# Thresholded attention into a tanh-shrink MLP on one core: rows 4p+c per partition, dense blocks by batch, output transposes later, weight casts behind their loads, threshold shift on VectorE

## The chip, the cores and the metric

One NeuronCore of a Trainium2 chip runs the whole program; the other cores are idle. The metric is the device time of one execution in microseconds (us), as the median of several runs. The engines are named as the profile names them: PE is the matrix engine (TensorE; PEld are its weight loads), DVE is VectorE, ACT is ScalarE, POOL is GpSimd, SP is the engine that issues most of the DMA transfers. Each engine works through its own queue in order, and semaphores tie the queues together.

## The reference, cut to what matters

```python
# q, k, v: 8 batches x 8 heads x 576 x 64, f32; tau = 0.02
scores = q @ k^T / 8                                # 576 x 576 for each head
thresh = max(scores, axis=-1) - tau
scores = where(scores >= thresh, scores, -1e9)
attn   = exp(scores - max(scores)); attn /= sum(attn) + 1e-9
x      = (attn @ v), heads side by side             # 4608 tokens x 512
h      = x @ w_in                                   # 512 -> 2048
out    = (h - tanh(h)) @ w_out                      # 2048 -> 512, f32
```

## The kernel before, in words

**Attention.** Two heads of a batch form a *pair*; there are 32 pairs, four to a batch. A pair has nine *tiles* of 128 query rows: four of the first head, a shared one with the last 64 rows of both heads (j = 4, kind "M"), four of the second. `load` brings q, k and v of a pair in f32; `split` turns q and k into a high and a low fp16 part (on POOL, for the first pair on ACT and DVE); `turn` transposes them on PE and copies the result from PSUM on DVE. For k a second matrix kS with the high and low halves swapped is made from kT by two DMAs.

For each tile: `scores` runs two groups of matmuls (with kT and kS) into one of two PSUM buffers, DVE scales the result into `sc` and takes the row maximum `mx`, POOL makes the shift `nb = tau - mx` (L226); `kink` on ACT (L240) applies a Prelu with a steep slope, which sends all below the threshold far down; `weights` transposes the result z on PE into the single PSUM buffer psZ (L256), and ACT takes the exponential into pT (L266); `attend` multiplies pT with v, on every second tile for two tiles at once, with a column of ones beside v that gives the row sums. `norm` (DVE, L314 and L315) divides, for the first head after tile 4 and for the second after tile 8, into `osb`. `emit_x` (L320) transposes `osb` on PE (psX, L324 and L331), in the same PSUM buffer as psZ, and DVE copies it into xT (L336).

**Dense layers.** Tokens are worked in nine blocks of 512. `hidden` computes 128 of the 2048 hidden columns for a block (four matmuls, tanh on ACT, the difference g on DVE); `project` adds a quarter of an output tile (four matmuls). `layers(m)` lists the 16 hidden steps of block m and the 16 projecting steps of block m-1.

**What sets the order.** There is no scheduler: the loop from L430 writes every engine's queue by hand. Step s does, in this order, the scores of tile s+3, the kink of s+1, the weights of s, then the dense steps that are due, `attend` of s-1, `norm`, `emit_x`, then loads, splits and turns of the next pair, and (in the first batch) a piece of the weights. At the first tile of the second and of each later batch a list of dense steps is taken up (16 in the first such batch, 32 in the later ones) and spread over the 36 tiles of the batch. In the first batch there are none. The last blocks run after the loop, without attention beside them: the tail.

The weights, 16 pieces of 128 x 1024 f32, go through two buffers: `w_load` issues the DMA and at once writes the cast to bf16 into POOL's queue (L417), one piece at each of the tiles 3 to 8 of a pair until all are there.

Of the kernel before, what the change touches and what calls it, by code (L numbers as in the profile page):

```python
# [10 lines left out]
BF16 = mybir.dt.bfloat16  # L11
# [7 lines left out]
def kernel(  # L19
# [32 lines left out]
    W = 2 * S  # L52
    AHEAD = 3

    MB = 512
    NMB = NT // MB
    MS = MB // P

    const = ctx.enter_context(tc.tile_pool(name="const", bufs=1))
    ident_f16 = const.tile([P, P], FP16, name="ident_f16")  # L60
# [1 line left out]
    ident_bf = const.tile([P, P], BF16, name="ident_bf")  # L62
    make_identity(nc, ident_bf)

    xT = const.tile([P, DM_C, NT], BF16, name="xT")
    w_in_sb = const.tile([P, DM_C, d_ff], BF16, name="w_in_sb")
    w_out_sb = const.tile([P, DF_C, d_model], BF16, name="w_out_sb")

# [36 lines left out]

    raws = {}

    def load(p):
        b, h0 = p // HPAIR, 2 * (p % HPAIR)
        for t, src in (("k", k), ("q", q)):  # L110
            r = raw_pool.tile([P, 10, D], F32, name=f"{t}raw", tag=t)
            for hh in range(2):
                nc.sync.dma_start(
                    out=r[:, 5 * hh : 5 * hh + 4, :],
                    in_=src[b, h0 + hh, 0:512, :].rearrange("(c p) d -> p c d", p=P),
                )
                nc.sync.dma_start(
                    out=r[64 * hh : 64 * hh + 64, 4, :], in_=src[b, h0 + hh, 512:S, :]
                )
            raws[p, t] = r  # L120
        r = raw_pool.tile([P, 10, D], F32, name="vraw", tag="v")
        for hh in range(2):
            nc.sync.dma_start(
                out=r[:, 4 * hh : 4 * hh + 4, :],
                in_=v[b, h0 + hh, 0:512, :].rearrange("(c p) d -> p c d", p=P),
            )
        rem = v[b, h0 : h0 + 2, 512:S, :].rearrange("h s d -> s h d")
        nc.sync.dma_start(out=r[0:64, 8:10, :], in_=rem)
        nc.sync.dma_start(out=r[64:P, 8:10, :], in_=rem)
        raws[p, "v"] = r  # L130
# [36 lines left out]
    def turn(p, t):  # L167
        hl = hls.pop((p, t))
        ps = ps_big.tile([P, W], FP16, name=f"ps_{t}", tag="big")
        for c in range(TPP):  # L170
            nc.tensor.matmul(  # L171
                out=ps[:, c * P : (c + 1) * P],
                lhsT=hl[:, c, :, :].rearrange("p a d -> p (a d)"),
                rhs=ident_f16, is_transpose=True, start=True, stop=True,
            )
        m = qk_pool.tile([P, W], FP16, name=f"{t}T", tag=t)
        nc.vector.tensor_copy(out=m, in_=ps)  # L177
        mats[p, t] = m
        if t == "k":
            sw = qk_pool.tile([P, W], FP16, name="kS", tag="ks")  # L180
            nc.sync.dma_start(out=sw[0:D, :], in_=m[D:P, :])
            nc.sync.dma_start(out=sw[D:P, :], in_=m[0:D, :])
            mats[p, "ks"] = sw
# [10 lines left out]
    def scores(i):  # L194
        p, j = divmod(i, TPP)
        qT, kT, kS = mats[p, "q"], mats[p, "k"], mats[p, "ks"]
        ps = ps_big.tile([P, 1024], F32, name="psS", tag="big")
        main, rem, lo = slice(0, 512), slice(512, 576), 0
        if kind(j) == "B":
            main, rem, lo = slice(512, 1024), slice(448, 512), 448  # L200
        if j == 4:
            for n, kk in enumerate((kT, kS)):
                for dst, srcs in ((main, MAIN), (rem, REM)):
                    for hh in range(2):
                        nc.tensor.matmul(  # L205
                            out=ps[64 * hh : 64 * hh + 64, dst],
                            lhsT=qT[:, REM[hh]], rhs=kk[:, srcs[hh]],
                            start=(n == 0), stop=(n == 1),
                        )
        else:  # L210
            hh = int(j > 4)
            lhs = qT[:, j * P : (j + 1) * P]
            for n, kk in enumerate((kT, kS)):
                for dst, src in ((main, MAIN[hh]), (rem, REM[hh])):
                    nc.tensor.matmul(  # L215
                        out=ps[:, dst], lhsT=lhs, rhs=kk[:, src],
                        start=(n == 0), stop=(n == 1),
                    )
        sc = sc_pool.tile([P, S], F32, name="sc")
        mx = st_pool.tile([P, 1], F32, name="mx", tag="mx")  # L220
        nc.vector.tensor_scalar(  # L221
            out=sc, in0=ps[:, lo : lo + S], scalar1=SC, scalar2=None,
            op0=ALU.mult, op1=ALU.max, accum_out=mx,
        )
        nb = st_pool.tile([P, 1], F32, name="nb", tag="nb")
        nc.gpsimd.tensor_scalar(  # L226
            out=nb, in0=mx, scalar1=-1.0, scalar2=tau, op0=ALU.mult, op1=ALU.add
        )
        scs[i] = sc, nb
# [90 lines left out]
    def emit_x(p):  # L320
# [12 lines left out]
                is_transpose=True, start=True, stop=True,  # L333
            )
        b = p // HPAIR
        nc.vector.tensor_copy(out=xT[:, p % HPAIR, b * S : (b + 1) * S], in_=ps)  # L336


    gs = {}
# [1 line left out]
    def hidden(m, n, ps):  # L341
        if n == 0:
            gs[m] = g_pool.tile([P, DF_C, MB], BF16, name="g")
        for c in range(DM_C):
            nc.tensor.matmul(  # L345
                out=ps, lhsT=w_in_sb[:, c, n * P : (n + 1) * P],
                rhs=xT[:, c, m * MB : (m + 1) * MB],
                start=(c == 0), stop=(c == DM_C - 1),
            )
        th = t_pool.tile([P, MB], F32, name="th")  # L350
        nc.scalar.activation(out=th, in_=ps, func=ACT.Tanh)  # L351
        nc.vector.scalar_tensor_tensor(  # L352
            out=gs[m][:, n, :], in0=th, scalar=-1.0, in1=ps,
            op0=ALU.mult, op1=ALU.add,
        )

    def project(m, ms, part, ps, last):
# [5 lines left out]
        if part == 3:  # L363
# [2 lines left out]
                nc.scalar.copy(out=yo, in_=ps)  # L366
            else:
                nc.vector.tensor_copy(out=yo, in_=ps)  # L368
            t0 = m * MB + ms * P
            nc.sync.dma_start(out=out[t0 : t0 + P, :], in_=yo)  # L370

    def layers(m, tail):

# [24 lines left out]
    def w_pieces():  # L398
        for w, sb, n in ((moe_w_in, w_in_sb, DM_C), (moe_w_out, w_out_sb, DF_C)):
# [3 lines left out]
            for i in range(8):  # L403
                yield flat, src, i, cols, w.shape[1]

    def w_load(piece):
        flat, src, i, cols, width = piece
        wt = wt_pool.tile([P, cols], F32, name="wt", tag="wt")
# [4 lines left out]
        else:  # L413
            r = width // cols
            s = src[:, i // r, (i % r) * cols : (i % r + 1) * cols]
            nc.sync.dma_start(out=wt, in_=s)
        nc.gpsimd.tensor_copy(out=flat[:, i * cols : (i + 1) * cols], in_=wt)  # L417


    load(0)  # L420
# [3 lines left out]
        turn(0, t)  # L424
    split_v(0)
    pieces = w_pieces()

    todo, stage = [], 0

    for s in range(-AHEAD, NTILE + 2):  # L430
        p, j = divmod(max(s, 0), TPP)
        if 0 <= s < NTILE and j == 0 and p % HPAIR == 0 and p >= HPAIR:
            assert not todo
            todo = layers(stage, False)
            share = len(todo) / (HPAIR * TPP)
            done, stage = 0.0, stage + 1
        if s + AHEAD < NTILE:
            scores(s + AHEAD)
# [2 lines left out]
        if 0 <= s < NTILE:  # L441
            weights(s)
            if todo:
# [3 lines left out]
                while todo and done >= 1:  # L447
                    todo.pop(0)()
                    done -= 1
        if 0 <= s - 1 < NTILE:  # L450
            attend(s - 1)
            pp, jj = divmod(s - 1, TPP)
# [1 line left out]
                norm(pp, 0)  # L454
            if jj == 8:
                norm(pp, 1)
                emit_x(pp)
        if 0 <= s < NTILE:
            if j == 0 and p + 2 < NPAIR:
                load(p + 2)  # L460
            if p + 1 < NPAIR:
# [6 lines left out]
                    turn(p + 1, "k")  # L468
                if j == 4:
                    turn(p + 1, "q")  # L470
            if p < HPAIR and j >= 3:
                piece = next(pieces, None)
                if piece:
                    w_load(piece)
# [42 lines left out]
```

## Time and profile before

| | |
|---|---|
| median of 3 runs | 702.17 us (701.99 to 703.81) |
| the profiled execution | 701.69 us, its span 699.9 us |
| PE busy | 609.4 us, 87% |
| ACT busy | 462.1 us, 66% |
| DVE busy | 422.5 us, 60% |
| POOL busy | 272.0 us, 39% |
| mean granted PE clock | 0.975 of full |

The span runs from the first to the last instruction. A busy time is the time in which an engine executed at least one instruction, over the whole span, so over stages with quite different limits; matmuls are pipelined and their ends are modelled, so that an engine with a busy share near 100% need not be at its peak. In a row of the order of time, what stands in brackets at the end is how long that engine had stood idle and what released it. In the rows of waits, the engine on the left stood still until the instruction on the right had ended; where an engine has nothing to do anyway, such a wait costs nothing.

### The profile page before, as it was taken

What the parts mean: (1) busy time and instruction counts of PE and PEld (TensorE: products, weight loads), DVE (VectorE), ACT (ScalarE), POOL (GpSimd) and SP (SyncE); (2) the same over time, 40 slices, a digit from 0 to 9 for tenths busy, and PEclk for the clock granted to TensorE, in tenths of its full rate; (3) what the DMA queues carried; (4) which work ended last, traced back from release to release, by engine and by line L of the source; (5) the groups of instructions that cost most, each with busy time, mean ns of one, the idle gap of its engine ahead of it and who ended that gap; (6) DMA issues with size and microseconds to landing.
All of it is one profiled execution on the core that took longest, in us unless ns stands there. A gap on an engine that the chain in (4) does not pass through costs nothing.

```text
span 699.9 us, 16371 instructions
## 1 busy us (share of the span) xinstructions
PE 609.4 (87%) x6112; PEld 366.5 (52%) x6112; DVE 422.5 (60%) x985; ACT 462.1 (66%) x761; POOL 272.0 (39%) x597
## 2 busy tenths in 40 slices
PE   1765688888999999999999999999999999999997
PEld 1443455555555555555555555555555555554443
DVE  1534456666666666666676766666666666654440
ACT  1555578777777777777777777777777777763330
POOL 2564655444444444433434344444444443200000
PEclk9978789999999999999999999999999999999999
DMA  5567643332133332323232333333332332100102
GB/s 118 134 182 215 180 95 85 72 70 63 27 86 85 87 85 72 78 72 86 69 78 68 83 84 87 85 85 88 85 81 67 83 77 54 33 16 31 46 30 76
DMA packets 134543, 57.70 MB, mean 82 GB/s; under 512 B 122688, under 2 KB 122688, under 8 KB 134464
## 3 DMA queue, kind: packets, MB, share of 16 engines
q1 hardware_dynamic: 134464, 56.66, 32.4%
q8 instruction: 48, 0.79, 0.5%
q14 instruction: 31, 0.25, 0.1%
HBM read 37.75 MB, written 9.44 MB: 67 GB/s over the span
## 4 chain that ended last, share of the span: by engine, by line
PE 69%; ACT 9%; DVE 8%; DMA 4%; issue 3%; POOL 3%; SPq 2%; POOLq 0%; DVEq 0%; ACTq 0%
PE psY L359 17%; PE psH L345 15%; PE psS L215 12%; PE psZ L256 9%; ACT th L351 3%; ACT pT L266 3%; PE psS L205 3%; ACT z L240 3%; PE psHt L345 2%; PE psO L300 2%; DVE yo L368 2%; DMA wt<-in_moe_w_in_dram 2%; PE ps_k L171 2%; PE psX L324 2%; DVE osb L315 2%
## 5 line engine op out<-in xcount | busy, mean ns | idle before, releaser
L266 ACT ACTIVATE pT<-psZ 128x512 f16<-128x512 bf16 (+1 forms) x288 | 184.2, 640 | 120.2 <-PE psZ L256 118.8
L240 ACT ACTIVATE z<-sc,nb 128x576 bf16<-128x576 f32 x288 | 221.5, 769 | 38.2 <-POOL nb L226 37.9
L221 DVE TENSOR_SCALAR_CACHE_REDUCE sc<-psS 128x576 f32<-128x576 f32 x288 | 214.9, 752 | 38.6 <-PE psS L215 15.6
L226 POOL TENSOR_SCALAR nb<-mx 128x1 f32<-128x1 f32 x288 | 54.8, 190 | 301.0 <-DVE sc L221 198.5
L352 DVE SCALAR_TENSOR_TENSOR g<-th,psH 128x512 bf16<-128x512 f32 x124 | 85.3, 688 | 114.5 <-ACT th L351 114.5
L359 PE MATMUL psY<-w_out_sb,g 128*128 128x512 bf16 x576 | 145.5, 379 | 0.0
L256 PE MATMUL psZ<-ident_bf,z 128*128 128x128 bf16 x1280 | 121.6, 223 | 27.0 <-ACT pT L266 25.5
L345 PE MATMUL psH<-xT,w_in_sb 128*128 128x512 bf16 x496 | 128.2, 381 | 0.5 <-DVE g L352 0.5
L256 PEld LDWEIGHTS <-z 128*128 128x128 bf16 x1280 | 80.8, 99 | 71.4 <-issue 28.7
L215 PE MATMUL psS<-kS,qT 128*128 128x512 f16 (+1 forms) x512 | 107.6, 293 | 5.3 <-DMA kS<-kT 5.2
L215 PE MATMUL psS<-kT,qT 128*128 128x512 f16 (+1 forms) x512 | 107.8, 293 | 3.6 <-DVE kT L177 1.9
L215 PEld LDWEIGHTS <-qT 128*128 128x128 f16 x1024 | 74.9, 99 | 63.9 <-issue 6.5
L351 ACT ACTIVATE th<-psH 128x512 f32<-128x512 f32 x124 | 74.0, 597 | 36.6 <-PE psH L345 36.4
L359 PEld LDWEIGHTS <-g 128*128 128x128 bf16 x576 | 51.3, 98 | 47.0
L345 PEld LDWEIGHTS <-w_in_sb 128*128 128x128 bf16 x576 | 51.6, 98 | 42.6 <-issue 1.4
L300 PEld LDWEIGHTS <-pT 128*128 128x128 f16 x1280 | 57.8, 100 | 24.7 <-issue 0.6
L300 PE MATMUL psO<-vb,pT 128*128 128x65 bf16 x1280 | 62.7, 196 | 0.0
L324 PE MATMUL psX<-ident_bf,osb 128*128 128x128 bf16 x128 | 13.3, 229 | 36.2 <-DVE osb L315 31.6
L149 POOL TENSOR_TENSOR qhl<-xs,qhl 128x576 f16<-128x576 f32 x31 | 39.7, 1279 | 2.6
L149 POOL TENSOR_TENSOR khl<-xs,khl 128x576 f16<-128x576 f32 x31 | 39.6, 1276 | 2.7
L177 DVE COPY qT<-ps_q 128x1152 f16<-128x1152 f16 x32 | 24.2, 757 | 20.3 <-PE ps_q L171 20.3
L177 DVE COPY kT<-ps_k 128x1152 f16<-128x1152 f16 x32 | 24.2, 757 | 18.5 <-PE ps_k L171 18.5
(50 smaller groups left out, 475.9 us busy)
## 6 DMA issues: line engine op xcount, KB each, us to landing
kS<-kT SPq DMA_DIRECT2D x64, 144.0 KB, 2.5
out_dram<-yo SPq DMA_DIRECT2D x36, 256.0 KB, 2.1
kraw<-in_k_dram SPq DMA_DIRECT2D x64, 128.0 KB, 2.5
qraw<-in_q_dram SPq DMA_DIRECT2D x64, 128.0 KB, 2.5
vraw<-in_v_dram SPq DMA_DIRECT2D x64, 128.0 KB, 2.6
wt<-in_moe_w_in_dram SPq DMA_DIRECT2D x8, 512.0 KB, 4.5
wt<-in_moe_w_out_dram SPq DMA_DIRECT2D x8, 512.0 KB, 4.1
vraw<-in_v_dram SPq DMA_DIRECT2D x64, 32.0 KB, 2.3
```

The source lines that it names most:

```text
L149: nc.gpsimd.tensor_tensor(out=hl[:, :, 1, :], in0=x, in1=hl[:, :, 0, :], op=ALU.subtract)
L215: nc.tensor.matmul(out=ps[:, dst], lhsT=lhs, rhs=kk[:, src], start=(n == 0), stop=(n == 1),)
L221: nc.vector.tensor_scalar(out=sc, in0=ps[:, lo : lo + S], scalar1=SC, scalar2=None, op0=ALU.mult, op1=ALU.max, accum_out=mx,)
L226: nc.gpsimd.tensor_scalar(out=nb, in0=mx, scalar1=-1.0, scalar2=tau, op0=ALU.mult, op1=ALU.add)
L240: nc.scalar.activation(out=z, in_=sc, func=ACT.Prelu, bias=nb, scale=1.0, alpha=STEEP)
L256: nc.tensor.matmul(out=ps[:, c * P : (c + 1) * P], lhsT=z[:, off + c * P : off + (c + 1) * P], rhs=ident_bf, is_transpose=True, start=True ...
L266: nc.scalar.activation(out=pt[:, off : off + n * P], in_=ps[:, 0 : n * P], func=ACT.Exp)
L300: nc.tensor.matmul(out=po[:, (j - 1 - 5 * hh) + ab, :], lhsT=pt[:, blk * P : (blk + 1) * P], rhs=vb[:, hh, c, :], start=(n == 0), stop=(n ...
L345: nc.tensor.matmul(out=ps, lhsT=w_in_sb[:, c, n * P : (n + 1) * P], rhs=xT[:, c, m * MB : (m + 1) * MB], start=(c == 0), stop=(c == DM_C - 1),
L351: nc.scalar.activation(out=th, in_=ps, func=ACT.Tanh)
L352: nc.vector.scalar_tensor_tensor(out=gs[m][:, n, :], in0=th, scalar=-1.0, in1=ps, op0=ALU.mult, op1=ALU.add,)
L359: nc.tensor.matmul(out=ps, lhsT=gs[m][:, n, ms * P : (ms + 1) * P], rhs=w_out_sb[:, n, :], start=(n == 0), stop=(n == DF_C - 1),)
```

## The change

Six edits.

1. **Rows.** A partition p takes rows 4p to 4p+3 of the first 512 rows of a head instead of rows p, p+128, p+256, p+384, so that a partition reads 1 KB in one run instead of four runs of 256 bytes. Both heads come by one DMA. q of the first pair is issued from ACT's queue. The order of the rows within a head changes for q, k and v alike.
2. **Blocks by batch.** Dense block m (m below 8) is the first 512 columns of batch m; block 8 is the last 64 columns of all eight batches. The output rows are written in the matching order.
3. **Output transposes.** `emit_x` of a pair is called after tile 1 of the next pair instead of after the pair's own tile 8. The dense steps of a batch start at its fourth tile and are spread over 33 tiles. Two steps are added to the end of the loop for the last pair.
4. **kS of the first pair** is made by 18 transposes on PE and a DVE copy instead of two DMAs.
5. **Weights.** A piece is loaded at every fourth tile from tile 3 on; its cast is written into POOL's queue four tiles later, just before the next load.
6. **`nb`** is computed on DVE.

```diff
@@ load
-            for hh in range(2):
-                nc.sync.dma_start(
-                    out=r[:, 5 * hh : 5 * hh + 4, :],
-                    in_=src[b, h0 + hh, 0:512, :].rearrange("(c p) d -> p c d", p=P),
-                )
...
+            eng = nc.scalar if p == 0 and t == "q" else nc.sync
+            eng.dma_start(
+                out=r.rearrange("p (h c) d -> p h (c d)", h=2)[:, :, 0 : 4 * D],
+                in_=src[b, hs, 0:512, :].rearrange("h (p c) d -> p h (c d)", c=4),
+            )
+            eng.dma_start(out=r[:, 4, :], in_=src[b, hs, 512:S, :])
@@ turn
-        if t == "k":
+        if t == "k" and p == 0:
+            ps = ps_big.tile([P, W], FP16, name="ps_ks", tag="big")
+            for c in range(TPP):
+                for a in range(2):
+                    nc.tensor.matmul(
+                        out=ps[64 * a : 64 * a + 64, c * P : (c + 1) * P],
+                        lhsT=hl[:, c, 1 - a, :],
+                        rhs=ident_f16, is_transpose=True, start=True, stop=True,
+                    )
+            sw = qk_pool.tile([P, W], FP16, name="kS", tag="ks")
+            nc.vector.tensor_copy(out=sw, in_=ps)
+            mats[p, "ks"] = sw
+        elif t == "k":
@@ scores
-        nc.gpsimd.tensor_scalar(
+        nc.vector.tensor_scalar(
             out=nb, in0=mx, scalar1=-1.0, scalar2=tau, op0=ALU.mult, op1=ALU.add
@@ hidden
-                rhs=xT[:, c, m * MB : (m + 1) * MB],
+                rhs=xT[:, c, m, 0:MB] if m < B else xT[:, c, :, MB:S],
@@ project
-            t0 = m * MB + ms * P
-            nc.sync.dma_start(out=out[t0 : t0 + P, :], in_=yo)
+            if m < B:
+                rows = out[m * S : m * S + MB, :].rearrange("(p c) n -> c p n", c=4)
+                nc.sync.dma_start(out=rows[ms], in_=yo)
+            else:
+                rows = out.rearrange("(b s) n -> b s n", b=B)
+                nc.sync.dma_start(out=rows[2 * ms : 2 * ms + 2, MB:S, :], in_=yo)
@@ w_load
-        nc.gpsimd.tensor_copy(out=flat[:, i * cols : (i + 1) * cols], in_=wt)
+        loaded.append((flat, wt, i, cols))
...
+    def w_cast():
+        flat, wt, i, cols = loaded.pop(0)
+        nc.gpsimd.tensor_copy(out=flat[:, i * cols : (i + 1) * cols], in_=wt)
@@ the loop
+    w_when = [4 * i + 3 for i in range(17)]
-    for s in range(-AHEAD, NTILE + 2):
+    for s in range(-AHEAD, NTILE + 4):
-        if 0 <= s < NTILE and j == 0 and p % HPAIR == 0 and p >= HPAIR:
+        if 0 <= s < NTILE and j == 3 and p % HPAIR == 0 and p >= HPAIR:
-            share = len(todo) / (HPAIR * TPP)
+            share = len(todo) / (HPAIR * TPP - 3)
+        if s - 1 == NTILE + 1:
+            emit_x(NPAIR - 1)
                 norm(pp, 1)
-                emit_x(pp)
+            if jj == 1 and pp > 0:
+                emit_x(pp - 1)
-            if p < HPAIR and j >= 3:
+            if s in w_when:
+                if loaded:
+                    w_cast()
                 piece = next(pieces, None)
```

How the queues change is seen at two places. The first is DVE's queue around the end of a pair in a full batch; rc and osb are `norm` of the second head, xT is the copy of the output transposes, sc the score reduction. Before:

```order
L221 TENSOR_SCALAR sc,mx<-psS 128x576
L368 COPY yo<-psY 128x512
L221 TENSOR_SCALAR sc,mx<-psS 128x576
L314 RECIPROCAL rc<-psO 128x4
L315 TENSOR_TENSOR osb<-psO,rc 128x4x64
L336 COPY xT<-psX 128x576
L221 TENSOR_SCALAR sc,mx<-psS 128x576
L352 SCALAR_TENSOR_TENSOR g<-th,psH 128x512
```

After, at the start of a batch:

```order
L327 RECIPROCAL rc<-psO 128x4
L328 TENSOR_TENSOR osb<-psO,rc 128x4x64
L234 TENSOR_SCALAR sc,mx<-psS 128x576
L239 TENSOR_SCALAR nb<-mx 128x1
L234 TENSOR_SCALAR sc,mx<-psS 128x576
L239 TENSOR_SCALAR nb<-mx 128x1
L349 COPY xT<-psX 128x576
L178 COPY kT<-ps_k 128x1152
```

The copy into xT, and the output transposes on PE with it, stood directly behind the norm; now two score reductions, each with its `nb`, stand between them, and the copy of kT comes right behind.

The second is POOL's queue in the first pair; xs, qhl, khl and vb belong to the splits of the next pair, w_in_sb to the cast of a piece of the weights. Before:

```order
L149 TENSOR_TENSOR qhl<-xs,qhl 128x9x64
L226 TENSOR_SCALAR nb<-mx 128x1
L156 CAST vb_76<-vraw 128x2x4x64
L160 CAST vb_76<-vraw 64x2x64
L161 CAST vb_76<-vraw 64x2x64
L226 TENSOR_SCALAR nb<-mx 128x1
L417 CAST w_in_sb<-wt 128x1024
L226 TENSOR_SCALAR nb<-mx 128x1
L417 CAST w_in_sb<-wt 128x1024
```

After:

```order
L150 TENSOR_TENSOR qhl<-xs,qhl 128x9x64
L157 CAST vb_76<-vraw 128x2x4x64
L161 CAST vb_76<-vraw 64x2x64
L162 CAST vb_76<-vraw 64x2x64
L427 CAST w_in_sb<-wt 128x1024
L146 TENSOR_SCALAR xs<-kraw 128x576
L149 CAST khl<-xs 128x9x64
```

Each tile's `nb` is gone from between the splits and the casts, and one cast is left in the first pair where there were six.

## Rows read from the trace of the kernel before

**Rows 1.** stretches: length, busy us (instructions) of each engine, clock, DMA
```profile
18.39:105.31 86.92, 59.79 (x632) 40.07 (x632) 41.98 (x107) 50.37 (x80) 50.11 (x93) 0.82 0.59 161
105.31:177.36 72.05, 59.86 (x684) 38.20 (x685) 48.29 (x116) 55.91 (x93) 31.96 (x73) 0.98 0.32 71
252.48:327.60 75.12, 69.96 (x749) 42.84 (x749) 51.07 (x120) 55.55 (x93) 32.30 (x73) 1.00 0.34 80
625.65:699.90 74.25, 69.87 (x326) 31.52 (x326) 26.25 (x39) 22.62 (x38) 0.00 (x0) 1.00 0.13 47
```

**Rows 2.** waits of PE, 106 to 627 us: total us, times, longest us
```profile
PE psX L324 <- DVE osb L315: 30.9, 28, 1.7
PE psZ L256 <- ACT pT L266: 10.1, 29, 0.4
```

**Rows 3.** order of time, 290 to 310 us: start, length, instruction [idle before]
```profile
290.32 0.40 PE L324 MATMUL psX<-ident_bf,osb 128*128 128x128 bf16 x4 [1.02 <-DVE osb L315]
...
290.91 0.46 DVE L336 COPY xT<-psX 128x576 bf16<-128x576 bf16 x1 [0.64 <-PE psX L331]
...
309.24 0.40 PE L324 MATMUL psX<-ident_bf,osb 128*128 128x128 bf16 x4 [1.02 <-DVE osb L315]
```

**Rows 4.** waits of the first batch, 18 to 106 us
```profile
ACT z L240 <- POOL nb L226: 37.9, 18, 12.5
...
POOL w_out_sb L417 <- DMA wt<-in_moe_w_out_dram: 10.1, 6, 2.3
...
POOL w_in_sb L417 <- DMA wt<-in_moe_w_in_dram: 8.8, 5, 2.5
```

**Rows 5.** order of time behind one cast of weights, 33 to 38.5 us
```profile
33.34 1.04 POOL L417 CAST w_in_sb<-wt 128x1024 bf16<-128x1024 f32 x1 [2.51 <-DMA wt<-in_moe_w_in_dram]
...
34.68 0.77 ACT L240 ACTIVATE z<-sc,nb 128x576 bf16<-128x576 f32 x1 [2.56 <-POOL nb L226]
...
37.84 0.69 PE L215 MATMUL psS<-kT,qT 128*128 128x512 f16 x2
```

**Rows 6.** order of time at the start, 0 to 23 us
```profile
7.86 1.14 PE L171 MATMUL ps_k<-ident_f,khl 128*128 128x128 f16 x9 [7.86 <-DVE khl L139]
...
9.04 0.76 DVE L177 COPY kT<-ps_k 128x1152 f16<-128x1152 f16 x1 [0.68 <-PE ps_k L171]
...
9.71 0.75 DVE L139 SCALAR_TENSOR_TENSOR qhl<-qraw,qhl 128x576 f16<-128x576 f32 x1
...
18.39 0.66 PE L215 MATMUL psS<-kS,qT 128*128 128x512 f16 x2 [5.22 <-DMA kS<-kT]
...
22.45 0.60 ACT L266 ACTIVATE pT<-psZ 128x512 f16<-128x512 bf16 x1 [0.55 <-PE psZ L256]
```

**Rows 7.** order of time in the fourth pair, 90 to 106 us
```profile
90.33 0.58 PE L324 MATMUL psX<-ident_bf,osb 128*128 128x128 bf16 x4 [2.04 <-ACT pT L266]
...
95.98 0.44 PE L256 MATMUL psZ<-ident_bf,z 128*128 128x128 bf16 x5
...
100.71 0.75 DVE L221 TENSOR_SCALAR_CACHE_REDUCE sc<-psS 128x576 f32<-128x576 f32 x1
...
100.72 0.70 ACT L266 ACTIVATE pT<-psZ 128x640 f16<-128x640 bf16 x1
...
101.39 0.75 DVE L221 TENSOR_SCALAR_CACHE_REDUCE sc<-psS 128x576 f32<-128x576 f32 x1
...
103.88 0.38 PE L256 MATMUL psZ<-ident_bf,z 128*128 128x128 bf16 x4 [0.33 <-ACT pT L266]
...
105.31 0.40 PE L324 MATMUL psX<-ident_bf,osb 128*128 128x128 bf16 x4 [0.74 <-DVE osb L315]
```

**Rows 8.** groups by line: count, busy us, mean ns, idle before
```profile
L226 POOL TENSOR_SCALAR nb<-mx 128x1 f32<-128x1 f32 x288 | 54.8, 190 | 301.0 <-DVE sc L221 198.5 <-ACT z L240 56.7 <-DVE rc L314 19.5
...
L221 DVE DVE_READ_ACCUMULATOR sc<-psS 128x1 f32 x288 | 23.9, 83 | 0.0
...
L314 DVE RECIPROCAL rc<-psO 128x4 f32<-128x4 f32 x32 | 5.6, 175 | 7.2 <-PE psO L300 7.2
```

More of the change, by code (lines that the diff above doesn't have):

```diff
@@ L55 @@
     MB = 512
-    NMB = NT // MB
-    MS = MB // P
+    NMB = B + 1
     const = ctx.enter_context(tc.tile_pool(name="const", bufs=1))
@@ L63 @@
     make_identity(nc, ident_bf)
-    xT = const.tile([P, DM_C, NT], BF16, name="xT")
+    xT = const.tile([P, DM_C, B, S], BF16, name="xT")
     w_in_sb = const.tile([P, DM_C, d_ff], BF16, name="w_in_sb")
@@ L109, in load @@
         b, h0 = p // HPAIR, 2 * (p % HPAIR)
+        hs = slice(h0, h0 + 2)
         for t, src in (("k", k), ("q", q)):
+            eng = nc.scalar if p == 0 and t == "q" else nc.sync
             r = raw_pool.tile([P, 10, D], F32, name=f"{t}raw", tag=t)
-            for hh in range(2):
-                nc.sync.dma_start(
-                    out=r[:, 5 * hh : 5 * hh + 4, :],
-                    in_=src[b, h0 + hh, 0:512, :].rearrange("(c p) d -> p c d", p=P),
-                )
-                nc.sync.dma_start(
-                    out=r[64 * hh : 64 * hh + 64, 4, :], in_=src[b, h0 + hh, 512:S, :]
-                )
+            eng.dma_start(
[3 more added lines that the diff above has]
+            eng.dma_start(out=r[:, 4, :], in_=src[b, hs, 512:S, :])
             raws[p, t] = r
         r = raw_pool.tile([P, 10, D], F32, name="vraw", tag="v")
[L122 to L127, printed above, removed]
+        nc.sync.dma_start(
+            out=r[:, 0:8, :].rearrange("p (h c) d -> p h (c d)", h=2),
+            in_=v[b, hs, 0:512, :].rearrange("h (p c) d -> p h (c d)", c=4),
+        )
+        rem = v[b, hs, 512:S, :].rearrange("h s d -> s h d")
         nc.sync.dma_start(out=r[0:64, 8:10, :], in_=rem)
@@ L178, in turn @@
         mats[p, t] = m
-        if t == "k":
+        if t == "k" and p == 0:
[6 more added lines that the diff above has]
+                        rhs=ident_f16, is_transpose=True, start=True, stop=True,
+                    )
+            sw = qk_pool.tile([P, W], FP16, name="kS", tag="ks")
+            nc.vector.tensor_copy(out=sw, in_=ps)
+            mats[p, "ks"] = sw
+        elif t == "k":
             sw = qk_pool.tile([P, W], FP16, name="kS", tag="ks")
@@ L335, in emit_x @@
         b = p // HPAIR
-        nc.vector.tensor_copy(out=xT[:, p % HPAIR, b * S : (b + 1) * S], in_=ps)
+        nc.vector.tensor_copy(out=xT[:, p % HPAIR, b, :], in_=ps)
     gs = {}
@@ L404, in w_pieces @@
                 yield flat, src, i, cols, w.shape[1]
+    loaded = []
+    def w_cast():
+        flat, wt, i, cols = loaded.pop(0)
+        nc.gpsimd.tensor_copy(out=flat[:, i * cols : (i + 1) * cols], in_=wt)
     def w_load(piece):
```

## The prediction

> **What bounds the kernel now.** I read the busy time by stage first, then the waits, then the order of time at three places. The table by stage [rows 1] falls into four parts. In the first batch (18.39 to 105.31 us, to the output transposes of its last pair), attention alone, no engine is near full: PE is busy 59.8 of 86.9 us at a granted clock of 0.82, ACT 50.4, DVE 42.0, POOL 50.1. In the second batch PE is busy 59.9 of 72.1. In a full batch, as from 252.48 to 327.60, it is busy 70.0 of 75.1 us, DVE 51.1, ACT 55.6: PE bounds it. In the tail only the dense layers are left, PE again, 326 matmuls in 74.25 us, 0.23 each.
>
> The waits say what the idle rest is. From 106 us on PE lost 30.9 us in 28 waits for the normalised output `osb`, and 10.1 us in 29 waits for exponentials [rows 2]. The row at 290.32 is one of the 28 [rows 3]: PE has come to the output transposes psX 1.02 us before DVE has written `osb`, and may do nothing that is queued behind them. The next pair's psX starts at 309.24, so a pair of heads takes 18.92 us. In the first batch ACT waited 37.9 us for the shift `nb` (12.5 of it at the start) while POOL waited 10.1 and 8.8 us for weights [rows 4]. The row at 33.34 shows how [rows 5]: a cast waits 2.51 us for its DMA, `nb` stands behind it in POOL's order, ACT's kink starts 2.56 us late, and PE, which has meanwhile stood still, runs at half rate at 37.84 (two groups of scores in 0.69 us).
>
> **The change part by part.** Sums are made against the profiled execution, 701.69 us (span 699.9, so 1.8 around it); the median of the runs shown, 702.17, is 0.5 above it.
>
> *Start.* PE now waits for the swapped copy kS by DMA until 18.39, 5.22 us [rows 6]. By transposes: PE is free at 9.00; 18 transposes at the 1.14/9 = 0.127 us of the row at 7.86 end at 11.3; the copy (0.76, as kT's) at 12.05; behind it on DVE the split of q (0.75) at 12.8; nine transposes at 13.95; qT's copy at 14.7; the first half of the scores (0.66) at 15.4 instead of 18.39: 3.0 us. k comes by two transfers instead of four, q on ACT's queue: no row prices that; bounds 0 and 1.5 us (a fifth of the 7.86); I take 0.5, near the lower end, since the bytes are the same. Sum -3.5.
> The Trainium skill ("DMA: Bandwidth & Descriptors", Issuing engines are not separate DMA queues) says that a second issuing engine saves only the time to issue; no run here shows that yet, and by it the 0.5 would be nearer to 0.
>
> *First batch.* With `nb` on DVE and the casts four tiles behind their loads, nothing on ACT's path stands behind POOL. What remains is the chain through the one psZ buffer: transposes, exponential, next transposes. The batch's fourth pair has no casts any more, and shows it [rows 7]: from the psZ at 95.98 to that at 103.88 six tiles take 7.90 us, 1.32 each, 11.9 for nine. The pair's psX goes through the same buffer, 290.32 to the end of xT's copy at 291.37, 1.05 us. With 0.3 for the k transposes, which those six tiles lack (an estimate), 13.2 us a pair. ACT (50.4/4 = 12.6 a pair, in part overlapping) and DVE (42.0/4 = 10.5 and nine `nb`) lie just below that. 4.1 us from the first scores to the first exponential at 22.45 [rows 6] and 4 x 13.2 make 56.9 instead of 86.9: -30.0. Bounds: 11.9 a pair (psX for nothing) gives -35.2; today's fourth pair, 90.33 to 105.31 or 14.98, gives -22.9.
>
> *The output transposes, two tiles later.* `osb` is then long written. 27 of the 28 waits go (-29.9); the last, 1.02 us, stays, since no tile follows the last pair.
> What is late next: psX still needs the psZ buffer, so it waits for the exponential of its own tile, and the next tile's transposes wait for xT's copy (0.46). In pairs that don't open a batch the dense step (four matmuls at 0.23) covers the first, and the nine transposes of `turn` with a set of scores the second. In the 7 that open one the dense steps now begin at the fourth tile, and the exponential (0.70 in the row at 100.72) is covered only in part. I take 0.08 us for 20 pairs and 0.75 for the 7: +7. Bounds: 0, and 29.9, everything handed back.
>
> *Dense steps on 33 tiles instead of 36.* 32 steps leave four tiles of a batch without one, before (spread) and after (three in a row and one). The waits of 0.35 us for an exponential stay in number: 0. It is the cover for psX that moves, counted above.
>
> *`nb` on DVE.* No row shows it. Below it lie 83 ns (reading the accumulator, 128x1), above it 175 ns (a reciprocal of 128x4) and 190 ns (the same operation on POOL) [rows 8]; it also waits for the accumulator, which today's next score reduction does not (they start 0.68 us apart at 100.71 and 101.39, though each lasts 0.75). At 0.2 us a tile DVE's 51.1 x 18.92/75.12 = 12.9 us a pair become 14.7, PE's pair being 17.8 after the change. Cost 0, hidden behind PE; what it is if DVE is too late for PE is the first rival. On POOL it frees 54.8 us that nobody waits for then.
>
> *The rest.* As many dense matmuls as before. Block 8 reads eight strips of 64 columns, and nothing like it is in the trace: 0, bounded by twice the time for its 64 matmuls, 64 x 0.23 = 14.7. Its output rows and the 1 KB runs move the same bytes, beside PE: 0. The casts of w_in end at tile 35 of 39, those of w_out at 67 of 75: 0, at worst one late load of some 5 us.
>
> Sum: -3.5 - 30.0 - 29.9 + 7 = -56.4; 701.7 - 56.4 = 645.3, with the 0.5 of the median 646 us.
>
> **The rivals.**
> *DVE is late next: 669.* PE's waits for `osb` go, but DVE works in order, and between the third and the fifth tile of a pair it now has xT, kT, qT, the norm and `nb` beside three reductions; PE waits for its score buffers instead. For: 14.7 of 17.8 us is 83%, and more in those tiles. Against: scores run three tiles ahead. Price: all 29.9 come back, 23 more than forecast.
> *Clock: 687.* The psZ chain leaves PE short gaps in every tile of the first batch. If the clock stays at the lower of its two levels (1.2 instead of 2.4 GHz) there, PE's 59.8 x 0.82 = 49 us become 98 and bound the batch: 98 - 57 = +41. Against: the half rate at 37.84 came behind a long stop [rows 5], and such stops go.
> The Trainium skill ("TensorE: Matmul & The Clock Gate", A second HAM failure mode: psum-queue depth-cycling) describes just such a loss: PE that idles briefly and often between groups while it cycles through PSUM buffers, with the clock falling and rising again. The 0.82 of the batch agrees that clock is lost, but the row that shows half rate has a long wait before it.
> *Block 8 reads at half rate: 661,* 14.7 more. Nothing speaks for it but that no row shows it.
> *DVE empties before `nb`, slower: 769.* If an instruction that waits for its forerunner on DVE starts only when that has wholly ended, `nb` costs its own 0.19 and up to the 0.75 of the reduction. At x us each, DVE's pair is 12.9 + 9x. It bounds the full pairs from (17.8 - 12.9)/9 = 0.54; against today's mean of (625.65 - 105.31)/28 = 18.58 us a pair, and 10.5 + 9x in the first batch, the kernel is slower than today from x = 0.71: 28 x (9x - 5.7) is then more than the 3.5 of the start and the 40.8 - 36x of the first batch. At 0.94 it is +67. Against: 0.19 is the dearest row of its kind, and the two reductions at 0.68 us overlap [rows 7].
> The Trainium skill ("VectorE: DVE Perf Modes", The DRAIN you can't avoid) states a flush after every DVE operation, about its duration less 266 ns. By it x would be some 0.68, DVE would bound the pairs at 19.0, and the time would be some 694 (an estimate from that page); the trace does not show the flush between reductions. I give it 0.02.
> *The waits only move: 702.* psX comes later but finds the buffer taken each time, and casts that wait for their load hold up POOL's splits and so the `turn`s. Against: no `nb` is left on POOL, whose work in the first batch, 50.1 of 86.9, shrinks.
>
> **How the numbers follow.** Forecast 646 with 0.69, its own range 637 to 658 (the bounds of the first batch, and psX at 0 to 0.7 us a pair); DVE late 0.13; clock 0.06; block 8 0.05; the flush 0.02; slower 0.03; no change 0.02. Below 636 I leave 0.05; above 670 lie the clock, the last three, and a little of the DVE rival, 0.15: the range is 636 to 670. A measurement of this kernel tells 0.3% (2.1 us) from no change: faster 0.95, same 0.02, slower 0.03.
>
> **What would show it.** In the waits after: psX waits for `osb` once, not 28 times; ACT waits for `nb` almost nowhere after the first tile; the first batch lasts 52 to 64 us at a clock near 1; a pair of a full batch takes 17.6 to 18.1 us; the first scores' second half starts by 16 us. The forecast is wrong if PE waits for score reductions or for xT by more than 10 us in all, if the first batch's clock stays near 0.8, or if `nb` with its wait holds DVE for over 0.5 us.

## The result and the profile after

| | before | after |
|---|---|---|
| median of 4 runs | 702.99 us (701.99 to 705.04) | 647.15 us (646.63 to 647.41) |
| profiled execution, span | 701.69 us, 699.9 us | 646.63 us, 644.8 us |

The ratio is 0.9201 (95%: 0.9177 to 0.9225). The forecast was 646 us in a range of 636 to 670. The total came out by luck: the tail lost 10.9 us that the forecast did not have, and the batches gained 10.2 us more than it said. From the page of after, each engine's busy time, its share of the span and its instructions:

```profile
PE   594.6 (92%) x6048; PEld 362.0 (56%) x6130; DVE 459.5 (71%) x1274; ACT 461.6 (72%) x761; POOL 215.2 (33%) x309
```

The stages of after, in the columns of [rows 1], which they answer line by line: the length; PE, PEld, DVE, ACT and POOL; the granted clock; the mean busy share of the 16 DMA engines; GB/s. They are the first batch, the second batch, a full batch and the tail; each batch ends with its last psX:

```profile
15.48:73.16 57.68, 51.20 (x665) 35.01 (x664) 48.60 (x153) 50.14 (x84) 31.95 (x44) 1.00 0.61 175
73.16:137.54 64.38, 57.98 (x675) 37.87 (x684) 52.33 (x150) 55.06 (x93) 41.85 (x58) 1.00 0.47 134
208.64:279.73 71.09, 69.51 (x738) 43.06 (x748) 55.60 (x157) 55.97 (x93) 25.20 (x36) 1.00 0.31 85
559.63:644.80 85.17, 69.51 (x319) 31.52 (x326) 26.24 (x39) 22.61 (x38) 0.00 (x0) 0.93 0.11 41
```

The first batch takes 57.7 us instead of 86.9 (and its last psX now comes two tiles later, so that two tiles more lie in it), a full batch 71.1 instead of 75.1; the clock is full in all three. The tail does the same 69.5 us of matmuls in 85.2 instead of 74.25 us: 10.9 us were lost there.

Waits of PE from 74 to 560 us, which answer [rows 2] (total us, times, longest):

```profile
PE psZ L269 <- ACT pT L279: 5.1, 17, 0.4
PE psX L337 <- ACT pT L279: 3.5, 7, 0.8
PE psH L358 <- issue: 1.3, 8, 0.2
PE psX L337 <- DVE osb L328: 1.0, 1, 1.0
PE psS L228 <- DVE kT L178: 0.5, 2, 0.2
PE psS L228 <- DVE sc L234: 0.3, 1, 0.3
```

The wait for `osb` is left once, as forecast, and little has come in its place: 3.5 us under psX, which are 0.8 once and 0.45 in each of six pairs that open a batch, 0.3 for score reductions, none for xT.

Where the time went stage by stage cannot be read from the psX rows alone, since psX itself now comes two tiles later. The copies of kT keep their place among the tiles. First and last of them in these stretches, before, then after:

```profile
110.17 0.75 DVE L177 COPY kT<-ps_k 128x1152 f16<-128x1152 f16 x1
...
595.90 0.76 DVE L177 COPY kT<-ps_k 128x1152 f16<-128x1152 f16 x1 [0.40 <-PE ps_k L171]
```

```profile
74.34 0.76 DVE L178 COPY kT<-ps_k 128x1152 f16<-128x1152 f16 x1
...
530.59 0.75 DVE L178 COPY kT<-ps_k 128x1152 f16<-128x1152 f16 x1
```

In the second batch's first pair after is 35.8 us ahead, in the last batch 65.3, at the last psX 66.0 (625.65 - 559.63), at the end 55.1. With the start (the first half that needs kS at 15.48 instead of 18.39, so 2.9 us) that splits the 55.1 us:

| term | forecast | measured |
|---|---|---|
| start | -3.5 | -2.9 |
| first batch | -30.0 | 35.8 - 2.9: -32.9 |
| batches 2 to 8: psX waits, less what is late next | -29.9 + 7 = -22.9 | 66.0 - 35.8: -30.2 |
| tail (output rows, block 8) | 0 | +10.9 |
| sum | -56.4 | -55.1 |

The tail of after in order of time, every copy into the output tile `yo` from 619 us on:

```profile
619.73 0.69 DVE L381 COPY yo<-psY 128x512 f32<-128x512 f32 x1 [3.00 <-PE psY L372]
...
623.23 0.58 ACT L379 COPY yo<-psY 128x512 f32<-128x512 f32 x1 [6.37 <-PE psY L372]
...
628.57 0.69 DVE L381 COPY yo<-psY 128x512 f32<-128x512 f32 x1 [8.15 <-DMA out_dram<-yo]
...
633.68 0.58 ACT L379 COPY yo<-psY 128x512 f32<-128x512 f32 x1 [9.87 <-DMA out_dram<-yo]
```

These belong to block 8, whose four output tiles go out as 2 x 64 rows of 512. The third of the four finds its buffer still being sent: the DMA issued behind the first, at about 620.4, has held it until 628.57, some 8 us, where an output tile of before landed in a median of 2.1 us. After the last copy only DMAs are left, from 634.3 to 644.8.

### The profile page after: what moved, and what is told of

It reads as the page before. It is cut to its first block, busy times and chain, and to the rows that moved or that the text cites. A ratio compares the mean times of both kernels' runs of the same rounds, so it can differ in the third digit from the quotient of the medians.

```text
span 644.8 us, 15693 instructions
## 1 busy us (share of the span) xinstructions
PE 594.6 (92%) x6048; PEld 362.0 (56%) x6130; DVE 459.5 (71%) x1274; ACT 461.6 (72%) x761; POOL 215.2 (33%) x309
## 4 chain that ended last, share of the span: by engine, by line
PE 79%; ACT 9%; DVE 4%; issue 3%; DMA 2%; SPq 1%; ACTq 0%
PE psY L372 18%; PE psH L358 16%; PE psS L228 16%; PE psZ L269 10%; PE psO L313 5%; ACT pT L279 5%; ACT z L253 3%; PE ps_k L172 3%; PE psHt L358 3%; PE ps_q L172 2%; PE psS L218 2%; DVE sc L234 2%; PE psX L337 2%; DMA out_dram<-yo 2%; PE psO L301 1%
## 5 line engine op out<-in xcount | busy, mean ns | idle before, releaser
L372 PE MATMUL psY<-w_out_sb,g 128*128 128x512 bf16 x540 | 138.2, 379 | 1.3
L269 PE MATMUL psZ<-ident_bf,z 128*128 128x128 bf16 x1280 | 118.8, 219 | 9.9 <-ACT pT L279 9.1
L358 PE MATMUL psH<-xT,w_in_sb 128*128 128x512 bf16 x451 | 118.1, 379 | 3.4 <-issue 1.3
L269 PEld LDWEIGHTS <-z 128*128 128x128 bf16 x1280 | 79.2, 98 | 52.2 <-issue 16.7
L228 PE MATMUL psS<-kT,qT 128*128 128x512 f16 (+1 forms) x512 | 105.8, 288 | 2.8 <-DVE qT L178 0.9
L228 PE MATMUL psS<-kS,qT 128*128 128x512 f16 (+1 forms) x512 | 105.6, 288 | 0.0
L146 POOL TENSOR_SCALAR xs<-kraw 128x576 f32<-128x576 f32 x31 | 20.8, 670 | 225.0 <-DMA kraw<-in_k_dram 159.1
L313 PEld LDWEIGHTS <-pT 128*128 128x128 f16 x1280 | 55.8, 98 | 22.4
L239 DVE TENSOR_SCALAR nb<-mx 128x1 f32<-128x1 f32 x288 | 44.3, 154 | 10.0
L328 DVE TENSOR_TENSOR osb<-psO,rc 128x320 bf16<-128x320 f32 x64 | 29.3, 458 | 2.2
```

What stands on the lines that cost most here:

```text
L228: nc.tensor.matmul(out=ps[:, dst], lhsT=lhs, rhs=kk[:, src], start=(n == 0), stop=(n == 1),)
L239: nc.vector.tensor_scalar(out=nb, in0=mx, scalar1=-1.0, scalar2=tau, op0=ALU.mult, op1=ALU.add)
L269: nc.tensor.matmul(out=ps[:, c * P : (c + 1) * P], lhsT=z[:, off + c * P : off + (c + 1) * P], rhs=ident_bf, is_transpose=True, start=True ...
L313: nc.tensor.matmul(out=po[:, (j - 1 - 5 * hh) + ab, :], lhsT=pt[:, blk * P : (blk + 1) * P], rhs=vb[:, hh, c, :], start=(n == 0), stop=(n ...
L358: nc.tensor.matmul(out=ps, lhsT=w_in_sb[:, c, n * P : (n + 1) * P], rhs=xT[:, c, m, 0:MB] if m < B else xT[:, c, :, MB:S], start=(c == 0), ...
L372: nc.tensor.matmul(out=ps, lhsT=gs[m][:, n, ms * P : (ms + 1) * P], rhs=w_out_sb[:, n, :], start=(n == 0), stop=(n == DF_C - 1),)
```

## The experiments

All were timed beside the kernel before (medians 703.2, 704.6 and 704.1 us in the three series, 703.0 in that of the result). So before moved by 1.6 us from series to series, and a difference to after of 1 or 2 us is not told from none by the times alone. Ratios are to before; each kernel is after with one edit, unless said.

### Block 8's output in two DMAs of 64 rows, or in two of half the columns

```
-                nc.sync.dma_start(out=rows[2 * ms : 2 * ms + 2, MB:S, :], in_=yo)
+                for hh in range(2):
+                    nc.sync.dma_start(
+                        out=rows[2 * ms + hh, MB:S, :], in_=yo[64 * hh : 64 * hh + 64, :]
+                    )
```

> The changed kernel; the output rows of block 8 go out in two transfers of 64 rows, one for each batch, instead of one transfer over two batches. Theory A: the transfer of shape 2 x 64 x 512 is spread over few DMA engines because its first dimension is 2, and so lasts 8 to 10 us; with 64 rows first it lasts 2 to 3 us as the others, and the 10.9 us that the tail had grown by come back: 636 to 638 us. Rival B: rows 4 x 64 apart in eight batches are slow to write wherever they come from: 646 to 648 us.

Measured: 637.32 us (637.17 to 638.14), 0.906 (0.9028 to 0.9093), 9.8 below after. The last three copies in order of time:

```profile
624.25 0.58 ACT L379 COPY yo<-psY 128x512 f32<-128x512 f32 x1 [6.37 <-PE psY L372]
...
627.66 0.69 DVE L381 COPY yo<-psY 128x512 f32<-128x512 f32 x1 [6.21 <-PE psY L372]
...
631.16 0.58 ACT L379 COPY yo<-psY 128x512 f32<-128x512 f32 x1 [6.32 <-PE psY L372]
```

No copy waits for a DMA. By this pace (6.91 us from the first row to the third) the last copy of after would have started at 623.23 + 6.91 = 630.14; it started at 633.68, 3.5 us late. The other 7.4 of the 10.9 lie behind the last copy: 10.5 us from its end to the end of the span, 3.2 in before.

```
+                for i in range(2):
+                    c = slice(256 * i, 256 * i + 256)
+                    nc.sync.dma_start(
+                        out=rows[2 * ms : 2 * ms + 2, MB:S, c], in_=yo[:, c]
+                    )
```

> The changed kernel; the same transfers of block 8 are split in two by columns, so that each is 2 x 64 x 256: twice the issues and half the bytes in each, but still 2 first. Theory A: still few engines, 646 to 650 us. Rival C (what helps is a smaller transfer, or more transfers in flight, not the dimension that stands first): 637 to 641 us.

Measured: 648.52 us, 0.9218 (0.9185 to 0.9252). Its waits in the tail:

```profile
ACT yo L379 <- DMA out_dram<-yo: 10.0, 1, 10.0
DVE yo L381 <- DMA out_dram<-yo: 8.0, 1, 8.0
```

As many DMAs of as many bytes as in the first kernel, and yet the waits stand. While only DMAs are left at the end, first in after, then in the kernel with one batch's 64 rows to a DMA (the columns of the stages):

```profile
634.30:644.80 10.50, 0.00 (x0) 0.00 (x0) 0.00 (x0) 0.00 (x0) 0.00 (x0) 0.50 0.11 44
...
631.80:635.60 3.80, 0.00 (x0) 0.00 (x0) 0.00 (x0) 0.00 (x0) 0.00 (x0) 0.95 0.32 69
```

A share of 0.11 (0.12 in the kernel with half the columns, from 635.3 us on) is that of about two of the 16 engines, 0.32 that of about five. And 44 GB/s for 10.5 us are some 460 KB, more than one tile of 256 KB, so two DMAs shared these engines. What counts is the shape: with half the columns the rows still go out as 2 x 64. The Trainium skill ("DMA: Bandwidth & Descriptors", Why a DMA increments its semaphore by 16 and not by 1) says that a DMA from SP or ACT is spread over the largest number of engines, up to 16, that divides the slowest dimension other than 1 of both of its patterns, here 2. Both runs agree with it, and so does the share of about two engines.

### The later output transposes undone, and alone

```
-    for s in range(-AHEAD, NTILE + 4):
+    for s in range(-AHEAD, NTILE + 2):
-        ... j == 3 and p % HPAIR == 0 and p >= HPAIR:
+        ... j == 0 and p % HPAIR == 0 and p >= HPAIR:
-            share = len(todo) / (HPAIR * TPP - 3)
+            share = len(todo) / (HPAIR * TPP)
-        if s - 1 == NTILE + 1:
-            emit_x(NPAIR - 1)
                 norm(pp, 1)
-            if jj == 1 and pp > 0:
-                emit_x(pp - 1)
+                emit_x(pp)
```

> The changed kernel with one edit undone: the output transposes stand directly behind the norm again, and the dense steps start at a batch's first tile. Theory: 27 waits of PE for the normalised output return, 30 us, and the few waits for the PSUM buffer go: 674 to 680 us. Rival: the later place only moved the wait and the gain of the full batches comes from the shift on DVE: 648 to 655 us.

Measured: 681.02 us (679.62 to 682.29), 0.9678 (0.9641 to 0.9715), 33.9 above after and 1 above the range expected. One row of its waits over the whole span, and two psX of a full batch:

```profile
PE psX L337 <- DVE osb L328: 35.0, 31, 1.8
```

```profile
257.73 0.40 PE L337 MATMUL psX<-ident_bf,osb 128*128 128x128 bf16 x4 [1.02 <-DVE osb L328]
...
276.65 0.40 PE L337 MATMUL psX<-ident_bf,osb 128*128 128x128 bf16 x4 [1.02 <-DVE osb L328]
```

The waits are back, and the pair takes 18.92 us as in [rows 3]. So the edit's worth, with all else in place, is about the whole of the waits.

The reverse, the same edit alone put into the kernel before:

> The kernel before with that one edit: output transposes two tiles later, dense steps on 33 tiles. Theory: the same 30 us come off alone, 671 to 675 us. Rival: with the shift still on POOL, behind the splits, ACT is late for the tiles at the start of a pair and gives part of it back: 680 to 690 us.

Measured: 687.08 us (684.96 to 690.62), 0.9755 (0.9707 to 0.9802): 16 us, where I had expected some 30. Waits over the whole span, and one of those for kS:

```profile
ACT z L240 <- POOL nb L226: 54.9, 35, 12.0
...
PE psZ L256 <- ACT pT L266: 23.5, 32, 3.0
...
PE psS L215 <- DMA kS<-kT: 16.7, 12, 5.6
PE psX L324 <- ACT pT L266: 8.5, 11, 2.2
```

```profile
238.38 0.42 PE L215 MATMUL psS<-kS,qT 128*128 128x512 f16 x2 [1.88 <-DMA kS<-kT]
```

The waits for `osb` went but for one, and in their place PE waited for kS by DMA: 16.7 us in 12, of which 5.6 is the wait at the start that before has too (5.2), so 11.1 in 11 are new. ACT waited longer for `nb` (37.9 in [rows 4]), as the rival had it, whose 680 to 690 us came out; kS stood in neither. So the edit gave its 30 only in a kernel where kS and `nb` follow; the next runs look for the edits that see to that.

### The shift on POOL again, the casts at once, and both

```
-        nc.vector.tensor_scalar(
+        nc.gpsimd.tensor_scalar(
             out=nb, in0=mx, scalar1=-1.0, scalar2=tau, op0=ALU.mult, op1=ALU.add
```

> The changed kernel with the shift nb back on POOL; casts stay four tiles behind their loads. Theory: nb then stands behind each pair's splits (2.6 us for k, 2.6 for q) and behind single casts, but no longer behind loads; ACT waits for it at the start of every pair, PE loses 0.5 to 1 us a pair: 665 to 680 us, part of it in the first batch. Rival: the casts alone were what held nb up, so that the place of nb hardly matters: 647 to 652 us.

Measured: 658.93 us (658.39 to 659.81), 0.9359 (0.9337 to 0.938), 11.8 above after; the size had been put too high. From 20 to 600 us ACT waits 28.2 us for it:

```profile
ACT z L253 <- POOL nb L239: 28.2, 27, 1.8
```

A pair of the first batch takes 14.6 us (psX at 50.42, 65.01 and 79.60) instead of 13.0. From copy of kT to copy of kT, the first batch is 6.8 us longer than in after, the second 2.6 and a full one 0.4. The second kernel casts each piece directly behind its load:

```
         loaded.append((flat, wt, i, cols))
+        w_cast()
```

> The changed kernel with each cast of weights written right behind its load again (at every fourth tile), nb on DVE. Theory: POOL still waits for the transfers, some 3 to 4 us each, but only splits stand behind it and they have slack: 646 to 650 us. Rival: the splits come late and with them the transposes of k and q, PE waits for POOL in the first two batches: 655 to 665 us.

Measured: 649.16 us (648.4 to 649.88), 0.9219 (0.9197 to 0.924), 2.0 above after, of which 1.5 can be seen in one pair of the first batch, 14.5 us instead of 13.0 (psX at 60.45 and 74.98). In order of time there:

```profile
61.66 1.04 POOL L427 CAST w_in_sb<-wt 128x1024 bf16<-128x1024 f32 x1 [3.30 <-DMA wt<-in_moe_w_in_dram]
...
65.48 0.68 PE L172 MATMUL ps_q<-ident_f,qhl 128*128 128x128 f16 x9 [1.36 <-POOL qhl L150]
```

With `nb` on DVE only the splits stand behind a late cast. Here the split of q followed a cast that had waited for its load, and PE waited for that split: what the rival had foreseen, but once and not batch by batch. Then both edits together:

> The changed kernel with both edits undone that the run with nb on POOL (658.9) and the run with casts at once (649.2) undid one at a time: nb on POOL and each cast right behind its load, still at every fourth tile. Theory: the two edits stand in for each other, since only nb behind a cast that waits for its load stops ACT; with both undone each of the 16 pieces stops it for 2 to 4 us, 25 to 45 us on top of the 658.9: 685 to 705 us. Rival: their costs add, 11.8 + 2.0: 660 to 663 us.

Measured: 674.22 us (673.86 to 675.44), 0.9579 (0.9565 to 0.9593). That is 27.1 above after, where the two alone sum to 13.8, and below what I expected. In order of time, in the first batch:

```profile
29.83 1.04 POOL L427 CAST w_in_sb<-wt 128x1024 bf16<-128x1024 f32 x1 [2.23 <-DMA wt<-in_moe_w_in_dram]
...
31.17 0.78 ACT L253 ACTIVATE z<-sc,nb 128x576 bf16<-128x576 f32 x1 [2.28 <-POOL nb L239]
...
32.59 0.58 PE L269 MATMUL psZ<-ident_bf,z 128*128 128x128 bf16 x4 [2.72 <-ACT pT L279]
```

This is the chain of [rows 5] again: cast, `nb`, kink, transposes, and PE slower behind it (0.58 instead of 0.38; the clock from 15 to 90 us is 0.93). Either edit breaks it, so each alone costs less to undo than the two together show.

### The loads: old rows, and only the old number of DMAs

```
-            eng.dma_start(
-                out=r.rearrange("p (h c) d -> p h (c d)", h=2)[:, :, 0 : 4 * D],
-                in_=src[b, hs, 0:512, :].rearrange("h (p c) d -> p h (c d)", c=4),
-            )
-            eng.dma_start(out=r[:, 4, :], in_=src[b, hs, 512:S, :])
+            for hh in range(2):
+                eng.dma_start(
+                    out=r[:, 5 * hh : 5 * hh + 4, :],
+                    in_=src[b, h0 + hh, 0:512, :].rearrange("(c p) d -> p c d", p=P),
+                )
+                eng.dma_start(
+                    out=r[64 * hh : 64 * hh + 64, 4, :], in_=src[b, h0 + hh, 512:S, :]
+                )
...
```

and v and the output rows likewise. That makes 12 loads a pair instead of 7, beside two DMAs for kS, in runs of 256 bytes.

> The changed kernel with the old rows: four runs of 256 bytes a partition and one transfer for each head, so 10 or 11 issues a pair on SP instead of 7 (7 output issues of a batch apart); blocks by batch and all other edits stay. Theory: in the run with the output transposes moved alone, PE lost 16.7 us in 12 waits for kS, because its two transfers stood in SP's order behind the loads of a pair; with the old loads these waits return: 655 to 665 us. Rival: bytes and issues are hidden beside PE, as the prediction had it: 646 to 649 us.

Measured: 660.15 us (658.96 to 661.99), 0.9369 (0.9341 to 0.9397), 13.0 above after. In order of time behind one copy of kT, and then the same place in after:

```profile
505.73 0.76 DVE L182 COPY kT<-ps_k 128x1152 f16<-128x1152 f16 x1
...
508.93 0.62 SPq L134 DMA_DIRECT2D vraw<-in_v_dram  x1
...
509.64 0.55 SPq L198 DMA_DIRECT2D kS<-kT  x1
...
513.93 0.42 PE L232 MATMUL psS<-kS,qT 128*128 128x512 f16 x2 [2.01 <-DMA kS<-kT]
```

```profile
494.25 0.76 DVE L178 COPY kT<-ps_k 128x1152 f16<-128x1152 f16 x1
...
495.04 0.51 SPq L194 DMA_DIRECT2D kS<-kT  x1
```

kT is ready at 506.5, but SP is still issuing loads, about 0.5 to 1 us each, and comes to kS at 509.64; the scores wait 2.01 us. In after SP has nothing else to issue and starts kS as the copy ends. To part the number of issues from the size of the runs, the next kernel keeps the 1 KB runs, `(p c) d -> p c d`, and the output rows of after, but loads head by head as above.

> The changed kernel with its rows (1 KB runs in HBM) but one transfer for each head, as before: 12 issues a pair on SP instead of 7 (the run with the old rows had 12 as well). Theory: it is the time to issue on SP that holds kS up, so PE waits for kS as with the old rows: 656 to 662 us. Rival: it is the 256-byte runs, which keep the DMA engines busy longer: 647 to 650 us.

Measured: 659.29 us (657.09 to 660.54), 0.9361 (0.9339 to 0.9382). One row of its waits from 74 to 570 us:

```profile
PE psS L232 <- DMA kS<-kT: 8.9, 9, 1.5
```

That is most of the 10.5 us by which its profiled execution is longer (span 655.3 against 644.8). It costs as much as the old rows: what the larger runs themselves give is under what can be told (660.15 against 659.29).

### kS of the first pair by DMA

```
-        if t == "k" and p == 0:
+        if False:
```

> The changed kernel with kS of the first pair made by two transfers again, behind the loads of two pairs in SP's order. Theory: the first scores' second half waits for it 2 to 4 us longer and all else is unchanged: 649 to 652 us. Rival: fewer loads stand ahead of it on SP than in the kernel before, so that the transfers come in time: 646 to 648 us.

Measured: 647.84 us (647.09 to 648.65), 0.9205 (0.919 to 0.922), not told from after. In order of time its kS, and then the start of after:

```profile
10.53 0.53 SPq L194 DMA_DIRECT2D kS<-kT  x1
...
13.97 0.67 PE L228 MATMUL psS<-kS,qT 128*128 128x512 f16 x2
```

```profile
10.03 1.17 PE L184 MATMUL ps_ks<-ident_f,khl 128*64 128x128 f16 x18
...
15.48 0.67 PE L228 MATMUL psS<-kS,qT 128*128 128x512 f16 x2
```

With 12 loads ahead of it on SP instead of the 24 of before (q of the first pair comes from ACT's queue), the swapped copy comes by DMA early enough, and its scores start 1.5 us sooner than by transposes; by the first psX 0.4 of that is left (33.73 against 34.16), and the end is the same. So beside the fewer issues of loads the transposes on PE buy nothing that can be told. No run has them alone: in the kernel with 12 loads a pair the scores with kS start at 15.70, but there q of the first pair comes from ACT's queue as well.

### A version that beats both

After, with block 8's output in two DMAs of 64 rows, the 64-row remainders of q and k loaded in two DMAs as well, both splits of pair 0 ahead of both of its `turn`s, and every second psZ of the first batch in the buffers of psH, which are free there:

```
+        if i < HPAIR * TPP and i % 2:
+            ps = ps_h.tile([P, 5 * P], BF16, name="psZ", tag="h")
+        else:
+            ps = ps_z.tile([P, 5 * P], BF16, name="psZ", tag="z")
```

> The changed kernel with four edits: block 8's output in two transfers of 64 rows; the last rows of q and k in two transfers of 64 rows; in the first batch psZ alternates between two PSUM buffers (that of the hidden steps is idle there); for the first pair both splits stand ahead of both turns. Theory: 637.3 from the first edit; first scores 1 to 3 us earlier; the first batch, 13.0 us a pair by the psZ chain, falls to ACT's own time, 12 us a pair, 3 to 4 us in all: 630 to 634 us. Rival: ACT alone already bounds the first batch: 634 to 637 us.

Measured: 630.70 us (629.93 to 630.94), 0.8955 (0.8935 to 0.8975). Two psX of its first batch:

```profile
42.64 0.38 PE L343 MATMUL psX<-ident_bf,osb 128*128 128x128 bf16 x4 [0.78 <-ACT pT L285]
...
54.38 0.39 PE L343 MATMUL psX<-ident_bf,osb 128*128 128x128 bf16 x4
```

Pairs there take 11.7 to 12.7 us instead of 13.0, and the first scores start at 12.35 instead of 15.00. 9.8 of the 16.4 us against after are the output (the first experiment); the other 6.6 were not parted.

## Why the prediction was right, and where it was not

*First batch: right in mechanism and size.* Waits of the first batch after, 15.48 to 73.16 us, which answer [rows 4], and a psX:

```profile
ACT z L253 <- DVE nb L239: 8.9, 2, 8.7
...
PE psZ L269 <- ACT pT L279: 4.0, 13, 0.3
```

```profile
60.16 0.38 PE L337 MATMUL psX<-ident_bf,osb 128*128 128x128 bf16 x4 [0.45 <-ACT pT L279]
```

The psZ chain bounds it: 13.00 us a pair (psX at 60.16 and 73.16, for one), where the forecast built 13.2 from [rows 7]; with psZ in two buffers, in the version that beats both, a pair takes 11.7 to 12.7. The clock was 1.00 there though PE waited 13 times, 0.3 us each, for the exponential before it: the rival of the clock falls. The waits of ACT for `nb` are gone (two are left, 8.7 of 8.9 us at the start). The reason was argued as one; the runs show two edits that in part stand in for each other: undoing `nb` costs 11.8, the casts 2.0, both 27.1. One row was misread: at 37.84 in [rows 5] stands one group of two matmuls, not two groups; its 0.69 us, against 0.41 for the same two at 36.63, still says that the clock was down by then.

*`nb` on DVE: right.* In order of time in a full batch, with the columns of before:

```profile
299.54 0.75 DVE L234 TENSOR_SCALAR_CACHE_REDUCE sc<-psS 128x576 f32<-128x576 f32 x1
300.21 0.08 DVE L234 DVE_READ_ACCUMULATOR sc<-psS 128x1 f32 x1
300.33 0.15 DVE L239 TENSOR_SCALAR nb<-mx 128x1 f32<-128x1 f32 x1
301.03 0.69 DVE L365 SCALAR_TENSOR_TENSOR g<-th,psH 128x512 bf16<-128x512 f32 x1 [0.54 <-ACT th L364]
```

`nb` ends 0.19 us behind the reduction, against the 0.2 assumed; DVE then has half a microsecond to spare. DVE is busy 55.6 of 71.1 us in a full batch, and PE waits 0.3 us in all for reductions: neither "DVE is late next" nor a flush between the two instructions is there.

*The output transposes: right in mechanism, the penalty mis-sized.* "I take 0.08 us for 20 pairs and 0.75 for the 7: +7": the seven lost 0.45 each, one other 0.8, the rest nothing, and PE never waited for xT. That is 4.0, and explains 3 of the 7.3 us by which batches 2 to 8 beat the forecast. A full batch gained 4.0 us, a pair taking 71.09/4 = 17.8 as forecast. A second term was put at nothing: the waits for an exponential were to stay in number, and fell from 29 with 10.1 us [rows 2] to 17 with 5.1. Together that is somewhat more than the 7.3; small new waits stand against it. The second batch gained 7.7 and not 4.0, and with this edit alone undone it takes 72.1 us again (kT at 77.17 and 149.29), so that too is the edit's: there before had 6.6 of its 30.9 us of waits for `osb`, in four.

*The output rows: the step that failed.* "Its output rows and the 1 KB runs move the same bytes, beside PE: 0" was wrong: the tail lost 10.9 us, and 9.8 came back with nothing but another shape of these DMAs. The bytes are the same, but block 8's DMA has another shape, and it is the last work of the kernel, where there is no PE to lie beside. That a 2 x 64 x 512 pattern takes 8 to 10 us no row of before showed; that is a reason to bound it, and I gave it no bounds. Block 8's strided reads, which I did bound, cost nothing that can be told: 69.51 us of matmuls against 69.87, and with the output in DMAs of 64 rows the tail takes 75.0 us (560.65 to 635.6) against 74.25.

*Start and 1 KB runs: the total near, the reason wrong.* I ascribed 3.0 us to the transposes on PE, and 0.5 to the fewer transfers. The 18 transposes took 1.17 us, half of what I had priced, but k came no sooner: its own transposes begin at 8.96 instead of 7.86. Beside the fewer loads, the transposes of kS bought nothing that can be told. The fewer issues free SP for kS, and through the whole kernel that is worth about 12 us once PE no longer waits for `osb`: with 12 loads a pair PE waits for kS 9 times, 8.9 us. With the old loads the later transposes alone met 11.1 us of such waits behind the start. I had given this edit 0 since I summed the edits against the waits of before, where kS was waited for once. So the rival "the waits only move" is half true of that edit alone, though they moved to kS and `nb` more than to the buffer that it named; other edits of the change kept it from coming true here.

*The sum* was right by luck: +10.9 in the tail and +0.6 at the start met -2.9 in the first batch and -7.3 in the others.

## What to carry to other kernels

Cost a moved DMA by the shape of its pattern and by what is left to do when it is issued, not by its bytes; above all the last one. Where a change takes away the wait that ends last, look at what each removed instruction was queued ahead of on every queue, SP's too: an edit that is worth nothing in the trace of before can decide how much of another edit's gain is kept. Undoing one edit at a time shows its worth with the others in place; two that break the same chain must be undone together as well.

## What the runs showed of the hardware that I had not expected

- An output tile of 128 rows went out in 8 to 10 us as 2 x 64 x 512, with its neighbour under way for part of that and about two of the 16 DMA engines busy (a share of 0.11 to 0.12); as two DMAs of 64 rows it no longer held anybody up (637.32 against 647.15 us). Halving its columns instead left the waits at 8.0 and 10.0 us.
- SP was busy some 0.4 to 1 us with issuing a load; with 12 loads a pair instead of 7, a small DMA behind them started 3 us late (509.64 against kT at 506.49), and the kernel took 12 us longer.
- 18 transposes of 64 columns took 1.17 us, 0.065 each, where nine of 128 columns took 1.14 (0.127 each), both at the start.
- Reading the accumulator and the `nb` that depends on it follow a reduction within 0.19 us.
